# Windowed attention feeding an ELU feed-forward layer: pieces of attention moved to other tiles of a chunk

## The chip, the cores and the metric

The kernel runs on one core of a Trainium2 chip. Its time is the device time of one execution in microseconds (us); the figure that is compared is the median over several runs. The engines of the core work side by side, each through its own instructions in order: PE (matrix products), DVE and POOL (elementwise work), ACT (functions and copies), SP (issues the transfers).

## What is computed

Eight batches of eight heads, 576 positions of 64 numbers each. Four heads attend to the last 32 positions, four to every fourth of the last 128. The attention's result, 4608 tokens of 512 numbers, goes through two matrix products with an ELU between them.

```python
scores = scale * np.matmul(q, k.transpose(0, 1, 3, 2))
scores = np.where(masks[None, :, :, :], scores, -1000000000.0)
scores = scores - np.max(scores, axis=-1, keepdims=True)
attn = np.exp(scores)
attn = attn / (np.sum(attn, axis=-1, keepdims=True) + 1e-09)
attn_out = np.matmul(attn, v)                       # (8, 8, 576, 64)
x = attn_out.transpose(0, 2, 1, 3).reshape(4608, 512)
h = x @ w_in                                        # 512 x 2048
g = np.where(h > 0.0, h, np.exp(np.minimum(h, 0.0)) - 1.0)
return g @ w_out                                    # 2048 x 512
```

## The kernel before

**Chunks and tiles.** The tokens are worked off in nine chunks of 512 (loop over `c`), the hidden layer in 16 tiles of 128 (loop over `f`). For one tile PE forms `h` (`gemm1`: 12 matmuls of 128x512; from chunk 1 on each operand is split into a rounded part and a remainder, `xh`/`xl` and `wh`/`wl`, and three of the four products are taken), then ACT and DVE make the ELU (`elu`, lines 324 to 342), then PE adds the tile's share of the output (`gemm2`, another 12 matmuls into four `o_ps` banks). `gemm2` runs two tiles behind `gemm1` (`LAG`).

**The ELU of a tile**, in the order of its dependences: ACT copies `h` out of its PSUM bank (L328), ACT takes the exponential (L330), DVE clamps (L336) and combines (L337), ACT rounds to `gh` (L340), DVE takes the remainder `gl` (L341). In chunks 1 to 6 there is one PSUM bank for `h` (`h0`), so the next tile's `gemm1` waits for the copy in L328; the bank `h1` takes results of attention.

**Attention beside it.** A batch has four pairs of heads. Chunk `c` reads tokens of batches `c-1` and `c` at most, so the attention of batch `c+1` is done beside chunk `c`. Batch 0 comes first of all and batch 1 beside chunk 0. From batch 2 on it comes in pieces (`piece`, line 277): at the tiles of a table, `when`, right behind the tile's `gemm1`, PE takes the output products of the pair before (24 small matmuls with `pt` and `vt`) and then the scores of the next pair (72 small matmuls with `kt` and `qt`). `probabilities` (line 245) makes of the scores, in this order: masked sum and maximum on DVE (L253 to L255), six exponentials on ACT, then, in a second step that is emitted one tile later (line 457), six more exponentials (all L259), the sum's reciprocal on DVE (L181, L182), the scaling on POOL (L183), and six transposes on DVE (L265) that fill `pt`. All of `pt` must be there before the output products of that pair can run, at the next piece. ACT copies these into `x32` (L173, L176). The last piece of a chunk completes the last pair of batch `c+1` and takes the scores of batch `c+2`'s first pair.

**Between chunks.** `split_x(c+1)` makes `xh` on ACT (L302) and `xl` on DVE (L303) out of `x32`, eight instructions on each engine. They write the same tiles that the chunk before reads, so the first can start when PE has used `xh` for the last time, in the last tile's `gemm1`, and the next chunk's first `gemm1` waits for them. Only one `gemm2` lies between. The first two `elu` of a chunk share ACT with the copies of the chunk before's output (`store`, L355), which empty the `o_ps` banks. In chunk 1, `split_w` splits weights beside the first tiles (L132 on DVE).

**The order of the work.** PE keeps the order in which the program is written. On ACT, DVE, POOL and SP a scheduler orders the instructions by its own estimate of when each can start; `tc.issue_after(x)` makes it put what follows no earlier than `x`. The order is fixed before the kernel runs.

Of the kernel before, what the change touches and what calls it, by code (L numbers as in the profile page):

```python
# [18 lines left out]
B, H, S, D = 8, 8, 576, 64  # L19
# [27 lines left out]
def body(ctx: ExitStack, tc: tile.TileContext, q, k, v, masks, w_in, w_out, out):  # L47
# [36 lines left out]
    def load_w(k, behind=None):  # L84

        raw[k] = wst.tile([P, 2, DM], I64, name=f"r{k % NR}")
        if behind is not None:
            nc.gpsimd.tensor_copy(out=raw[k].bitcast(F32)[:QB, :, 0:1], in_=behind[:, 0:2].unsqueeze(2))
        for t in range(2):
            i = need[2 * k + t]  # L90
            nc.sync.dma_start(out=raw[k][:, t, :], in_=(w_in, w_out)[i % 2][i // 2])
# [6 lines left out]
    def magnitude(k):  # L98
        pair = full2[k] = wst.tile([P, 2, DM], F32, name=f"a{k}")
        for t in range(2):  # L100
            full[need[2 * k + t]] = pair[:, t, :]
        return nc.scalar.activation(out=pair.rearrange("p t c -> p (t c)"), in_=halves(k)[1].bitcast(F32), func=AF.Abs)

    def convert(k, keep=lambda ins: ins, part=slice(0, 2 * DM)):

        lo, hi = [u[:, part] for u in halves(k)]
        a = full2[k].rearrange("p t c -> p (t c)")[:, part]
        au = a.bitcast(U32)

        keep(nc.vector.tensor_scalar(out=a, in0=a, scalar1=TINY, scalar2=None, op0=ALU.max))  # L110

        keep(nc.vector.tensor_scalar(out=au, in0=au, scalar1=0x07FFFFFF, scalar2=3, op0=ALU.bitwise_and, op1=ALU.logical_shift_left))  # L112
        keep(nc.vector.scalar_tensor_tensor(out=au, in0=hi, scalar=0xC0000000, in1=au, op0=ALU.bitwise_and, op1=ALU.bitwise_or))  # L113

        return keep(nc.vector.scalar_tensor_tensor(out=au, in0=lo, scalar=29, in1=au, op0=ALU.logical_shift_right, op1=ALU.bitwise_or))  # L115

    def split_w(k):

        if k >= K0:
            both = wst.tile([P, 2, 2, DM], F32R, name=f"r{k - K0}")  # L120
            h, l = both[:, 0, :, :], both[:, 1, :, :]
        else:
            l = wst.tile([P, 2, DM], F32R, name=f"a{k - 1}")
            slot = NF - K0 + k // 2
            if slot < NR:
                if k % 2 == 0:
                    split_w.room = wst.tile([P, 2, 2, DM], F32R, name=f"r{slot}")
                h = split_w.room[:, k % 2, :, :]
            else:
                h = wst.tile([P, 2, DM], F32R, name=f"a{K0 + k - 2 * (NR - NF + K0)}")  # L130
        nc.scalar.copy(out=h, in_=full2[k])  # L131
        nc.vector.tensor_tensor(out=l, in0=full2[k], in1=h.bitcast(F32), op=ALU.subtract)  # L132
        for t in range(2):
            wh[need[2 * k + t]], wl[need[2 * k + t]] = h[:, t, :], l[:, t, :]
# [157 lines left out]
    def split_x(c):  # L292
        for hp in range(NC):
            xh[hp] = xp.tile([P, TC], F32R, name=f"xh{hp}")
            xl[hp] = xp.tile([P, TC], F32R, name=f"xl{hp}")
            t0 = c * TC
            while t0 < (c + 1) * TC:
                b, o = divmod(t0, S)
                n = min(S - o, (c + 1) * TC - t0)
                u = slice(t0 - c * TC, t0 - c * TC + n)  # L300
                src = x32[b][:, hp, o:o + n]
                nc.scalar.copy(out=xh[hp][:, u], in_=src)  # L302
                nc.vector.tensor_tensor(out=xl[hp][:, u], in0=src, in1=xh[hp][:, u].bitcast(F32), op=ALU.subtract)  # L303
                t0 += n
# [14 lines left out]
    def gemm1(c, f):  # L319
        for h_ps in first if (c, f) == (0, 0) else product1(c, f):  # L320
            pass
        return h_ps

    def elu(h_ps, first):
        e = fp.tile([P, TC], F32, name="e", bufs=3)
        if not first:
            h = fp.tile([P, TC], F32, name="h", bufs=1)
            freed.append(nc.scalar.copy(out=h, in_=h_ps).ins)  # L328
            h_ps = h
        nc.scalar.activation(out=e, in_=h_ps, func=AF.Exp)  # L330
        if first:
            below.append(nc.scalar.activation(out=e, in_=e, func=AF.Relu, scale=-1.0, bias=1.0).ins)
            g = fp.tile([P, TC], F32, name="gh", bufs=3)
            hidden.append(nc.vector.scalar_tensor_tensor(out=g, in0=h_ps, scalar=0.0, in1=e, op0=ALU.max, op1=ALU.subtract).ins)
            return g, None
        nc.vector.tensor_scalar(out=e, in0=e, scalar1=1.0, scalar2=-1.0, op0=ALU.min, op1=ALU.add)  # L336
        hidden.append(nc.vector.scalar_tensor_tensor(out=e, in0=h_ps, scalar=0.0, in1=e, op0=ALU.max, op1=ALU.add).ins)  # L337
        gh = fp.tile([P, TC], F32R, name="gh", bufs=3)
        gl = fp.tile([P, TC], F32R, name="gl", bufs=2)
        nc.scalar.copy(out=gh, in_=e)  # L340
        nc.vector.tensor_tensor(out=gl, in0=e, in1=gh.bitcast(F32), op=ALU.subtract)  # L341
        return gh, gl
# [15 lines left out]
    def batch_attention(b):  # L358

        x32[b] = xp.tile([P, NPAIR, S], F32, name="x32", bufs=2)  # L360

        old = None
        for hp in range(NPAIR):
            *_, new = probabilities(b, hp, loaded_pairs.pop((b, hp)), banks())
            yield
            if old is not None:
                outputs(*old[:2], [(a, i * NA, (i + 1) * NA) for i, a in enumerate(banks())], *old[2:])
                yield
            old = new
        outputs(*old[:2], [(a, i * NA, (i + 1) * NA) for i, a in enumerate(banks())], *old[2:])  # L370
        yield
# [45 lines left out]
    def flush(n):  # L417
        while len(pend) > n:
            c, f, g = pend.pop(0)
            if f == 0:  # L420
                o_of[c] = [ps_o.tile([P, DM], F32, name="o_ps") for _ in range(TC // P)]
            gemm2(o_of[c], g, f)
            if f == NF - 1:
                store(c, o_of.pop(c))

    for c in range(NCH):
        if c == 1:
            with tc.issue_after(hidden[F0 - 4]), tc.issue_after(below[F0 - 4]):
                split_x(c)
        elif c > 1:  # L430
            split_x(c)
        att = batch_attention(c + 1) if c == 0 else iter(())

        when = () if c == 0 or c >= B - 1 else (0, 4, 7, 11, 14) if c == 1 else (2, 6, 10, 14)
        emitted = 0
        for f in range(NF):
            while c == 0 and ready < min(NF, f + AHEAD):
                with tc.issue_after(below[-1] if below else last_copy.ins):
                    magnitude(ready)
                with tc.issue_after(last_conversion.ins):  # L440
                    last_conversion = convert(ready)
                if ready + NR < NF:
                    load_w(ready + NR)
                ready += 1
            if c == 0 and f == F0 - 4:
                with tc.issue_after(hidden[-1]), tc.issue_after(below[-1]):
                    split_x(0)
            if c == 0 and K0 <= f + 2 < NF:
                with tc.issue_after(hidden[-1]):
                    split_w(f + 2)  # L450
            while c == 1 and split < min(K0, f + 2):

                with tc.issue_after(hidden[NF - 4 if split < 2 else NF - 1]):
                    split_w(split)
                split += 1
            pend.append((c, f, elu(gemm1(c, f), c == 0 and f < F0)))
            if steps is not None:

                with tc.issue_after(freed[-1]):
                    current, steps = next(steps), None  # L460
            if f in when:
                n = (c + 1) * NPAIR + when.index(f) + NPAIR + 1 - len(when)
                current, steps = None, piece(current, divmod(n, NPAIR) if n < B * NPAIR else None)
            while emitted < (f + 1) * STEPS // (NF - 1):
                emitted += 1
                if c == 0 and emitted <= 2:
                    with tc.issue_after(last_step[NPAIR - 1]):
                        next(att, None)
                else:
                    next(att, None)  # L470
            flush(LAG)
# [60 lines left out]
```

## Time and profile before

| | |
|---|---|
| time, median of 3 runs | 922.26 us (921.44 to 922.37) |
| the profiled execution's own time | 921.04 us |
| its span, first to last instruction | 919.3 us |
| PE busy | 889.4 us (97%) |
| DVE busy | 553.1 us (60%) |
| ACT busy | 463.2 us (50%) |
| POOL busy | 45.9 us (5%) |
| mean granted PE clock | 0.996 |
| a tile's `gemm1` or `gemm2`, 12 matmuls, on the chain of waits | 2.72 us |

A row of the timeline reads: start in the span, duration (both us), engine, line of the program, operation, what it writes and reads, shapes, the number of instructions merged in the row, and in brackets how long the engine stood idle before it and what ended that. A row of waits reads: who waited, for whom, the total in us, how many times, the longest. A row of stretches reads: the stretch in us, its length, the busy time and instructions of PE, PE's weight loads, DVE, ACT and POOL, the granted PE clock, the transfers' share and GB/s. Chunk 2 begins at 242.56 us, chunk 6 at 637.88, chunk 7 at 735.84.

### The profile page before, as it was taken

The page shows a single profiled execution, that of the slowest core. Times are in us where ns is not written, and L with a number is a line of the kernel's source. Part 1 is how long each engine was busy: PE and PEld are TensorE (multiplying, and loading weights), DVE is VectorE, ACT ScalarE, POOL GpSimd, SP SyncE. Part 2 cuts the span into 40 slices and gives each one's busy share as a digit, 9 for nine tenths or more (in the row PEclk, how much of TensorE's full clock was granted, in tenths as well). Part 3 has the DMA queues.
Part 4 walks back from the last instruction along what each step waited for, and adds up shares of the span by engine and source line. Part 5 has one row for each costly group of instructions (what it writes and reads, how often), then busy time and mean ns, then how long its engine had stood idle before and what let it go on. Part 6 is the DMA issues. An engine that isn't in the chain of part 4 may idle for free.

```text
span 919.3 us, 16120 instructions
## 1 busy us (share of the span) xinstructions
PE 889.4 (97%) x6536; PEld 694.0 (75%) x6536; DVE 553.1 (60%) x926; ACT 463.2 (50%) x1317; POOL 45.9 (5%) x36
## 2 busy tenths in 40 slices
PE   6899999999999999999999999999999999999998
PEld 4444467788788877888788878887888888888886
DVE  5999989675755565666655665556555633343332
ACT  4754596455555455444644465455554443344333
POOL 2000000100000000000000000000000000000000
PEclk8999999999999999999999999999999999999999
DMA  9963111111121112111111112111200010001001
GB/s 348 404 231 116 44 36 57 60 45 45 45 90 45 45 44 91 45 45 45 55 37 44 46 44 90 45 44 45 90 19 1 1 47 1 0 1 47 1 1 46
DMA packets 23803, 59.40 MB, mean 65 GB/s; under 512 B 2640, under 2 KB 2736, under 8 KB 23728
## 3 DMA queue, kind: packets, MB, share of 16 engines
q1 hardware_dynamic: 23728, 58.37, 18.7%
q8 instruction: 51, 0.84, 0.4%
q14 instruction: 24, 0.20, 0.1%
HBM read 48.92 MB, written 9.44 MB: 63 GB/s over the span
## 4 chain that ended last, share of the span: by engine, by line
PE 77%; DVE 10%; ACT 6%; DMA 3%; issue 2%; SPq 1%; DVEq 0%; ACTq 0%
PE h L82 38%; PE o_ps L82 36%; PE a_ps L82 3%; ACT sm L259 2%; DMA r<-w_out 2%; DVE a L115 1%; ACT xh L302 1%; DVE a L113 1%; DVE e L336 1%; ACT r L131 1%; DMA kt<-k 1%; DVE a L110 1%; DVE pt L265 1%; DMA vt<-v 1%; DVE a L112 1%
## 5 line engine op out<-in xcount | busy, mean ns | idle before, releaser
L82 PE MATMUL o_ps<-a,gh 128*128 128x512 f32 x576 | 205.7, 426 | 0.0
L82 PE MATMUL o_ps<-r,gh 128*128 128x512 f32 x576 | 193.1, 394 | 1.6 <-ACT o L355 1.3
L340 ACT CAST gh<-e 128x512 fp32r<-128x512 f32 x132 | 82.2, 623 | 221.2 <-DVE e L337 221.2
L82 PE MATMUL h<-xh,r 128*128 128x512 f32 x512 | 183.6, 393 | 5.5 <-ACT xh L302 4.4
L336 DVE TENSOR_SCALAR e<-e 128x512 f32<-128x512 f32 x132 | 62.8, 475 | 161.8 <-ACT e L330 159.7
L82 PE MATMUL h<-xl,r 128*128 128x512 f32 x368 | 143.9, 391 | 5.8 <-DVE xl L303 5.8
L82 PE MATMUL h<-xh,a 128*128 128x512 f32 x480 | 147.8, 389 | 0.0
L82 PE MATMUL o_ps<-r,gl 128*128 128x512 f32 x368 | 143.5, 390 | 1.5 <-DVE gl L341 1.5
L328 ACT COPY h<-h 128x512 f32<-128x512 f32 x132 | 77.1, 584 | 133.2 <-PE h L82 133.2
L82 PEld LDWEIGHTS o_ps<-a,gh 128*128 128x128 f32 x576 | 107.3, 188 | 39.0 <-issue 19.6
L259 ACT ACTIVATE sm<-sm,nmx 96x64 f32<-96x64 f32 x336 | 112.4, 337 | 42.2 <-DVE nmx L255 42.2
L341 DVE TENSOR_TENSOR gl<-e,gh 128x512 fp32r<-128x512 f32 x132 | 91.4, 692 | 69.5 <-ACT gh L340 56.5
L82 PEld LDWEIGHTS o_ps<-r,gh 128*128 128x128 f32 x576 | 107.5, 188 | 25.8 <-ACT o L355 1.7
L82 PEld LDWEIGHTS h<-xh,r 128*128 128x128 f32 x512 | 96.1, 188 | 28.4 <-ACT xh L302 6.5
L337 DVE SCALAR_TENSOR_TENSOR e<-h,e 128x512 f32<-128x512 f32 x132 | 112.0, 849 | 4.3
L82 PEld LDWEIGHTS h<-xh,a 128*128 128x128 f32 x480 | 90.1, 188 | 18.7
L330 ACT ACTIVATE e<-h 128x512 f32<-128x512 f32 x144 | 90.4, 628 | 21.2 <-PE h L82 18.7
L265 DVE STREAM_TRANSPOSE pt<-sm 32x384 f32<-32x384 f32 x168 | 95.4, 568 | 1.9
L82 PEld LDWEIGHTS h<-xl,r 128*128 128x128 f32 x368 | 69.1, 188 | 22.4 <-DVE xl L303 7.7
L82 PEld LDWEIGHTS o_ps<-r,gl 128*128 128x128 f32 x368 | 69.1, 188 | 16.7 <-DVE gl L341 1.9
L183 POOL TENSOR_TENSOR sm<-sm,sums 96x768 f32<-96x768 f32 x24 | 39.9, 1661 | 654.7 <-ACT e L330 403.2
L259 ACT ACTIVATION_READ_ACCUMULATOR sm<-sm,nmx 96x1 f32 x336 | 63.3, 188 | 0.0
(92 smaller groups left out, 764.1 us busy)
## 6 DMA issues: line engine op xcount, KB each, us to landing
vt<-v SPq DMA_DIRECT2D x30, 384.0 KB, 3.2
kt<-k SPq DMA_DIRECT2D x30, 304.0 KB, 4.6
qt<-q SPq DMA_DIRECT2D x30, 288.0 KB, 4.2
r<-w_in SPq DMA_DIRECT2D x16, 512.0 KB, 7.9
r<-w_out SPq DMA_DIRECT2D x16, 512.0 KB, 8.2
out<-o SPq DMA_DIRECT2D x32, 256.0 KB, 2.2
out<-xl SPq DMA_DIRECT2D x4, 256.0 KB, 2.1
r<-v SPq DMA_DIRECT2D x2, 384.0 KB, 8.4
```

What stands on the lines that cost most here:

```text
L82: inorder(nc.tensor.matmul(*args, **kw))
L110: keep(nc.vector.tensor_scalar(out=a, in0=a, scalar1=TINY, scalar2=None, op0=ALU.max))
L112: keep(nc.vector.tensor_scalar(out=au, in0=au, scalar1=0x07FFFFFF, scalar2=3, op0=ALU.bitwise_and, op1=ALU.logical_shift_left))
L183: return keep(eng.tensor_tensor(out=sm, in0=sm, in1=sums.unsqueeze(2).broadcast_to([QB, 2 * NU, 2 * G]), op=ALU.mult))
L259: nc.scalar.activation(out=sm[:, u, :], in_=sm[:, u, :], func=AF.Exp, bias=nmx[:, u:u + 1], scale=0.125, accum_out=sums[:, u:u + 1])
L265: nc.vector.transpose(out=tr[ks, :, cs], in_=sm[cs, :, rs])
L328: freed.append(nc.scalar.copy(out=h, in_=h_ps).ins)
L330: nc.scalar.activation(out=e, in_=h_ps, func=AF.Exp)
L336: nc.vector.tensor_scalar(out=e, in0=e, scalar1=1.0, scalar2=-1.0, op0=ALU.min, op1=ALU.add)
L337: hidden.append(nc.vector.scalar_tensor_tensor(out=e, in0=h_ps, scalar=0.0, in1=e, op0=ALU.max, op1=ALU.add).ins)
L340: nc.scalar.copy(out=gh, in_=e)
L341: nc.vector.tensor_tensor(out=gl, in0=e, in1=gh.bitcast(F32), op=ALU.subtract)
```

## The change

The table of tiles changes: in chunk 1 from 0, 4, 7, 11, 14 to 0, 4, 7, 10, 12, and in chunks 2 to 6 from 2, 6, 10, 14 to 2, 5, 9, 12. The second step of chunk 1's first piece is emitted at tile 2 in place of tile 1. No instruction is added or dropped.

```diff
@@ -431,7 +431,7 @@
-        when = () if c == 0 or c >= B - 1 else (0, 4, 7, 11, 14) if c == 1 else (2, 6, 10, 14)
+        when = () if c == 0 or c >= B - 1 else (0, 4, 7, 10, 12) if c == 1 else (2, 5, 9, 12)
@@ -454,7 +454,7 @@
             pend.append((c, f, elu(gemm1(c, f), c == 0 and f < F0)))
-            if steps is not None:
+            if steps is not None and (c, f) != (1, 1):
 
                 with tc.issue_after(freed[-1]):
                     current, steps = next(steps), None
```

**ACT where chunk 1 meets chunk 2.** `xh` rows are the split for chunk 2, `sm` rows exponentials of the last piece, the `h` row the copy of tile 15. Before:

```order
 L340 CAST gh<-e 128x512
 L259 ACTIVATE sm,sums<-sm,nmx 96x64 x6
 L302 CAST xh_2346<-x_557 128x128
 L302 CAST xh_2346<-x_1582 128x384
 L302 CAST xh_2352<-x_557 128x128
 L302 CAST xh_2352<-x_1582 128x384
 L302 CAST xh_2358<-x_557 128x128
 L302 CAST xh_2358<-x_1582 128x384
 L328 COPY h<-h_2290 128x512
 L259 ACTIVATE sm,sums<-sm,nmx 96x64 x6
 L302 CAST xh_2364<-x_557 128x128
```

Now, on the same engine at the same place:

```order
 L340 CAST gh<-e 128x512
 L302 CAST xh_2346<-x_557 128x128
 L302 CAST xh_2346<-x_1582 128x384
 L302 CAST xh_2352<-x_557 128x128
 L302 CAST xh_2352<-x_1582 128x384
 L302 CAST xh_2358<-x_557 128x128
 L302 CAST xh_2358<-x_1582 128x384
 L328 COPY h<-h_2311 128x512
 L302 CAST xh_2364<-x_557 128x128
 L302 CAST xh_2364<-x_1582 128x384
 L330 ACTIVATE e<-h 128x512
```

Both groups of exponentials have left; they stand beside tiles 12 and 13 now. The same holds where chunks 2 to 6 begin the next one, but for the end of chunk 6, whose last piece has no scores.

**ACT in chunk 1 between its last two pieces.** The `sm` rows are the exponentials of the last piece but one, the `x` row at the end copies out the products of that same pair, which need its `pt`. Before, tiles 11 to 14:

```order
 L259 ACTIVATE sm,sums<-sm,nmx 96x64 x6
 L330 ACTIVATE e<-h 128x512
 L340 CAST gh<-e 128x512
 L328 COPY h<-h_2154 128x512
 L330 ACTIVATE e<-h 128x512
 L340 CAST gh<-e 128x512
 L328 COPY h<-h_2189 128x512
 L173 COPY x_1582<-a_ps_2212 128x96
```

Now, tiles 10 to 12:

```order
 L259 ACTIVATE sm,sums<-sm,nmx 96x64 x6
 L330 ACTIVATE e<-h 128x512
 L340 CAST gh<-e 128x512
 L328 COPY h<-h_2119 128x512
 L330 ACTIVATE e<-h 128x512
 L173 COPY x_1582<-a_ps_2142 128x96
```

One tile's ELU fewer stands between the exponentials and the copy of the products that depend on them.

**ACT in the first tiles of chunk 1.** The `o` row empties the output banks of chunk 0; the second `sm` row before is the moved step. Before:

```order
 L259 ACTIVATE sm,sums<-sm,nmx 96x64 x6
 L330 ACTIVATE e<-h 128x512
 L259 ACTIVATE sm,sums<-sm,nmx 96x64 x6
 L355 COPY o<-o_ps 128x512 x4
 L340 CAST gh<-e 128x512
 L328 COPY h<-h_1476 128x512
 L330 ACTIVATE e<-h 128x512
```

Now:

```order
 L259 ACTIVATE sm,sums<-sm,nmx 96x64 x6
 L330 ACTIVATE e<-h 128x512
 L355 COPY o<-o_ps 128x512 x4
 L340 CAST gh<-e 128x512
 L328 COPY h<-h_1455 128x512
 L259 ACTIVATE sm,sums<-sm,nmx 96x64 x6
 L330 ACTIVATE e<-h 128x512
```

The second six exponentials have moved behind the output copies, tile 1's `gh` and the copy of tile 2's `h`.

**DVE in the same tiles**, from tile 1's `gl` to tile 2's `gl`; the transposes are the first piece's. Before:

```order
 L341 TENSOR_TENSOR gl<-e,gh 128x512
 L336 TENSOR_SCALAR e<-e 128x512
 L265 STREAM_TRANSPOSE pt_79<-sm 32x12x32 x6
 L337 SCALAR_TENSOR_TENSOR e<-h,e 128x512
 L341 TENSOR_TENSOR gl<-e,gh 128x512
```

Now:

```order
 L341 TENSOR_TENSOR gl<-e,gh 128x512
 L181 TENSOR_SCALAR sums<-sums 96x12
 L182 RECIPROCAL sums<-sums 96x12
 L336 TENSOR_SCALAR e<-e 128x512
 L337 SCALAR_TENSOR_TENSOR e<-h,e 128x512
 L265 STREAM_TRANSPOSE pt_79<-sm 32x12x32 x6
 L341 TENSOR_TENSOR gl<-e,gh 128x512
```

The six transposes have moved from ahead of tile 2's L337 to behind it, and the sum's reciprocal from ahead of tile 1's `gl` to behind it.

## The prediction

> **What bounds the kernel now.** PE is busy for 889.4 of 919.3 us, so a move of work between the other engines can only change what PE waits. I read the list of PE's waits first (us in total, times, longest):
>
> ```profile
> PE h L82 <- DVE xl L303: 5.8, 5, 1.2
> PE h L82 <- ACT xh L302: 4.4, 5, 0.9
> PE o_ps L82 <- ACT o L355: 1.3, 1, 1.3
> PE h L82 <- ACT h L328: 1.1, 1, 1.1
> ```
>
> Ten waits at the starts of `gemm1` are for `xh` and `xl`, so they lie where chunks meet; the two single ones lie in chunk 1. The timeline shows a meeting of chunks, 5 with 6:
>
> ```profile
> 637.88 0.39 PE L82 MATMUL h<-xh,r 128*128 128x512 f32 x1
> 640.27 0.49 PE L82 MATMUL h<-xh,r 128*128 128x512 f32 x1 [0.87 <-ACT xh L302]
> 641.96 0.50 PE L82 MATMUL h<-xl,r 128*128 128x512 f32 x1 [1.20 <-DVE xl L303]
> 643.23 0.62 PE L82 MATMUL o_ps<-r,gh 128*128 128x512 f32 x2
> ...
> 637.00 0.35 ACT L259 ACTIVATE sm<-sm,nmx 96x64 f32<-96x64 f32 x1
> 639.00 0.50 ACT L302 CAST xh<-x 128x384 fp32r<-128x384 f32 x1
> ```
>
> Chunk 6's first `gemm1` lasts from 637.88 to 643.23, 5.35 us, with 2.07 us of waits in it. The six exponentials of the last piece's second step (from 637.00) stand on ACT ahead of the last casts to `xh` (from 639.00), for which PE waits. Chunk 6's own last piece has no scores, and so no exponentials. Where it meets chunk 7 the same rows read:
>
> ```profile
> 735.84 0.39 PE L82 MATMUL h<-xh,r 128*128 128x512 f32 x1
> 738.56 0.62 PE L82 MATMUL o_ps<-r,gh 128*128 128x512 f32 x2
> ...
> 732.64 1.94 ACT L302 CAST xh<-x 128x448 fp32r<-128x448 f32 x6 [3.02 <-PE h L82]
> 734.48 0.58 ACT L328 COPY h<-h 128x512 f32<-128x512 f32 x1
> 734.96 0.71 ACT L302 CAST xh<-x 128x448 fp32r<-128x448 f32 x2
> ...
> 735.56 0.76 DVE L303 TENSOR_TENSOR xl<-x,xh 128x448 fp32r<-128x448 f32 x2 [0.22 <-ACT xh L302]
> ```
>
> That `gemm1` takes 738.56 - 735.84 = 2.72 us. With ACT free, the casts begin 3.20 us ahead of it, and the last `xl` ends at 736.32, well before PE's eighth matmul, which reads it. So a meeting loses 5.35 - 2.72 = 2.63 us, and for 2.07 us of idle time in the list. Scaled to the list's 10.2 us over five meetings (into chunks 2 to 6), 10.2 x 2.63 / 2.07 = 13.0 us are lost.
>
> **The meetings of chunks.** The last piece moves from tile 14 to 12. What its chain does with four free tiles behind it is seen on chunk 6's piece beside tile 10:
>
> ```profile
> 703.46 0.97 PE L82 MATMUL a_ps<-kt,qt 64*32 64x64 f32 x72
> 723.55 0.39 PE L82 MATMUL h<-xh,r 128*128 128x512 f32 x1
> ...
> 707.12 0.35 ACT L259 ACTIVATE sm<-sm,nmx 96x64 f32<-96x64 f32 x1 [1.55 <-DVE nmx L255]
> 710.69 0.35 ACT L259 ACTIVATE sm<-sm,nmx 96x64 f32<-96x64 f32 x1
> 720.87 0.62 ACT L340 CAST gh<-e 128x512 fp32r<-128x512 f32 x1 [3.42 <-DVE e L337]
> 721.39 0.58 ACT L328 COPY h<-h 128x512 f32<-128x512 f32 x1
> ...
> 713.42 1.68 POOL L183 TENSOR_TENSOR sm<-sm,sums 96x768 f32<-96x768 f32 x1 [22.37 <-ACT e L330]
> ...
> 713.81 1.84 DVE L337 SCALAR_TENSOR_TENSOR e<-h,e 128x512 f32<-128x512 f32 x1
> 715.57 3.47 DVE L265 STREAM_TRANSPOSE pt<-sm 32x384 f32<-32x384 f32 x6
> 719.08 0.69 DVE L341 TENSOR_TENSOR gl<-e,gh 128x512 fp32r<-128x512 f32 x1
> ```
>
> From the start of the scores (703.46) the first exponentials follow at 3.66 us, the second six at 7.23, POOL's scaling at 9.96, the transposes from 12.11 to 15.58; the rounding to `gh` two tiles on comes at 17.41, ACT's next instruction at 17.93, and the `gemm1` of the tile four further on at 20.09. For a piece beside tile 12, "four further on" is the next chunk's first tile and the `gh` is tile 14's, behind which the order now has the casts. So they start at 17.93, 2.16 us ahead of that `gemm1`, not 3.20 as into chunk 7: the transposes hold DVE until 15.58, and with it tile 14's ELU. From the first cast, chunk 7's rows give 734.48 + 0.58 - 732.64 = 2.42 us to the end of tile 15's copy of `h` and 736.32 - 732.64 = 3.68 us to the last `xl`. That is 20.35 and 21.61. The single `h0` bank is then free 0.3 us late; the eighth matmul, 7 x 0.227 = 1.59 us after the start (2.72 / 12 each), finds its `xl`. I keep 0.3 us a meeting: 5 x 0.3 = 1.5 us stay, **11.5 us go**. The ends: all 13.0 go (as into chunk 7), or none (as now).
>
> **The gaps of three tiles.** From tile 2 to 5 and from 9 to 12 pieces now follow each other after three tiles in place of four, in chunk 1 from 7 to 10 too. Chunk 1 has such a gap from 4 to 7 already:
>
> ```profile
> 171.90 0.97 PE L82 MATMUL a_ps<-kt,qt 64*32 64x64 f32 x72
> ...
> 189.36 0.39 PE L82 MATMUL a_ps<-pt,vt 128*64 128x96 f32 x4
> ...
> kt<-k SPq DMA_DIRECT2D x30, 304.0 KB, 4.6
> ```
>
> From the scores to the next piece pass 17.46 us. The chain wants 15.58, so 1.88 us are spare, and no wait of PE on `pt` stands in that place in the list. I cost the twelve gaps at nothing; what covers them is two tiles' matmuls, and each us by which the chain grew over 1.88 would cost a us in each. No transfer is added; a pair's loads on SP's queue go out with the piece before, land in a median of 4.6 us (last row, the slowest of the three), and keep at least two tiles, 10.9 us. POOL has one scaling a pair, as before.
>
> **The gap of two tiles.** Chunk 1's last two pieces stand beside tiles 10 and 12. A tile is 2 x 2.72 = 5.44 us, so from the scores to the next piece pass 17.46 - 5.44 = 12.02 us, where the chain wants 15.58. PE's output products wait for the last transpose, and PE, in order, holds everything behind them: scores, `gemm2`, the next `gemm1`. That is a new **stall of 3.6 us**, late for all that follows. Nothing in the order shortens it: the same waits for tile 11's copy of `h`, for POOL (L337 takes 1.84 us beside it) and for six transposes remain. Without every wait it would be 3.66 + 4.0 for twice six exponentials (12 x 0.33) + 0.4 for L181 and L182 + 1.68 + 3.47 = 13.2, a stall of 1.2, which is the low end.
>
> **The clock.** Near the start PE once stood idle for about as long:
>
> ```profile
> 14.26 2.19 PE L82 MATMUL c<-ident,sm 96*64 96x96 f32 x24 [3.57 <-DVE sm L183]
> ...
> 9.10:12.51 3.41, 1.59 (x93) 1.04 (x81) 3.05 (x6) 1.69 (x2) 0.18 (x1) 1.00 1.05 415
> 12.51:15.93 3.42, 1.67 (x22) 1.71 (x24) 3.35 (x5) 0.36 (x1) 0.18 (x1) 0.50 1.02 400
> 15.93:19.34 3.41, 3.41 (x91) 2.44 (x90) 3.25 (x7) 3.09 (x10) 1.91 (x2) 0.50 1.05 393
> 244.62:248.03 3.41, 1.85 (x7) 1.31 (x8) 3.40 (x5) 0.90 (x2) 1.25 (x1) 1.00 0.02 5
> ```
>
> These are stretches between changes of the granted clock (the column before the last two). In the first, PE was busy for 1.59 of 3.41 us, 47%; then the clock was 0.50 for two stretches, the second of them fully busy, and 1.00 again. A stretch 54% busy at 244.62 left it at 1.00. If the limit lies between, a stall of 3.6 us is enough wherever it falls: split evenly over two stretches it leaves 1.8 us idle in each, 47% busy. Then a stretch of 3.41 us runs at half speed, which costs 1.7 us less half of what the stall itself still fills of it, 0 to 1.8 us. I take **1.3 us**; the ends are 0 and 3.4 (two stretches).
>
> By the Trainium skill (TensorE: Matmul & The Clock Gate, "Part 1: The HAM clock gate") the clock falls only after about 3.4 us in which PE idles a whole window. By that a 3.6 us stall fills a window in 1 of 20 positions and this term is 0 as a rule, the time 912.4. The row at 9.10 speaks against it, since the clock fell after a window that was not idle.
>
> **The first tiles of chunk 1.**
>
> ```profile
> 155.61 0.33 ACT L259 ACTIVATE sm<-sm,nmx 96x64 f32<-96x64 f32 x1
> 157.60 2.00 ACT L355 COPY o<-o_ps 128x512 f32<-128x512 f32 x4
> ...
> 158.08 0.68 DVE L337 SCALAR_TENSOR_TENSOR e<-h,e 128x512 f32<-128x512 f32 x1
> 162.39 3.47 DVE L265 STREAM_TRANSPOSE pt<-sm 32x384 f32<-32x384 f32 x6
> ...
> 158.22 0.50 PE L82 MATMUL o_ps<-r,gh 128*128 128x512 f32 x1 [1.29 <-ACT o L355]
> 167.77 0.50 PE L82 MATMUL h<-xh,r 128*128 128x512 f32 x1 [1.08 <-ACT h L328]
> ```
>
> The second six exponentials start at 155.61 and the output copies behind them at 157.60, so `o_ps` came late (1.29 us). Moved behind, they let the copies start at 155.61, and the first, 0.62 us long to PE's start, is done before PE asks at 158.22 - 1.29 = 156.9: that wait goes. Tile 1's `gh` is then bound by L337, which ends at 158.76; 0.52 us later (as 720.87 to 721.39) ACT copies `h`, to 159.9, where PE, which goes on from 156.8, wants the bank at 156.8 + 2.72 = 159.5: 0.4 stay. The exponentials follow 0.5 us into that copy, at 159.8, and from there the chain above holds: L337 of tile 2 ends 715.65 - 710.69 = 4.96 us later, at 164.8, no longer behind transposes that end at 165.86. Then `gh` and, 0.52 later, the copy of `h` to 165.9, where PE wants the bank at 165.4: 0.5 stay. Tile 4's `gemm1` starts at 165.95, not 167.77. With the shorter restart **2.0 us go**. The transposes end 8.35 us after 159.8, at 168.2, and the piece beside tile 4 begins at 165.95 + 2.81 = 168.8: 0.6 to spare. The ends: 0 and 2.4 (both waits whole).
>
> **The sum**, against the profiled execution's own 921.04 us: -11.5 - 2.0 + 3.6 + 1.3 = -8.6, so 912.4. The median of the runs shown is 1.2 above that execution, so the forecast is **913.7 us** (47%).
>
> **The rivals.**
>
> *The clock holds* (25%). As forecast without the 1.3: 912.4 us. For it: beside the stall stand matmuls of 512 columns, where the idle time at 14.26 lay among small ones; against it the 47% above. The Trainium skill's rule on the clock gate (TensorE: Matmul & The Clock Gate, Part 1) gives this time.
>
> *The chain closes up* and the stall beside tile 12 is at its low end, 1.2 us, too short for the clock (a stretch stays 65% busy): 922.26 - 11.5 - 2.0 + 1.2 = 910.0 us (10%). Against it: ACT waits for PE's tile 11 between the two sixes, whatever else moves.
>
> *The casts slide further* (12%). If tile 14's ELU comes another us later (DVE holds it behind transposes), each meeting keeps 1.3 us: 913.7 + 5 = 918.7. For it: the slack of the last `xl` is only 21.99 - 21.61 = 0.4.
>
> *Slower: the chain outgrows three tiles* (4%). The place is the output products beside tiles 5 and 12 of chunks 2 to 6, ten new gaps. It decides from a chain longer than 17.46; to eat the 8.6 us and 1.8 more it must cost 1.0 us in each, a chain of 18.5 against 15.58: 913.7 + 10.4 = 924.1. For it: L337 already stretches from 0.68 to 1.84 us beside POOL; against it, the gap of 4 to 7 ran without a wait.
>
> *The meetings stay as they are* (2%), PE waiting for the bank instead of for `xl`: 13.0 remain, chunk 1's 2.0 go and 4.9 come: 925.2, or 921.5 with the stall at its low end.
>
> **Range and chances.** 910.3 to 917.8 us holds the forecast, the clock that holds, and the nearer part of the casts and of the closed-up chain. About 0.2%, 1.8 us, is what a measurement of this kernel can tell from no change. Faster by more 0.94, within it 0.02, slower 0.04.
>
> **What would show it.** Right: the list of PE's waits without the pair for `xh` and `xl`; first `gemm1` of chunks 2 to 6 about 3.0 us long or beginning 0.3 us late behind an ACT `h`; one wait of some 3.6 us of `a_ps` on DVE `pt` beside chunk 1's tile 12, and a second row of granted clock 0.5 soon after it; no wait on `pt` in chunks 2 to 6. Wrong: waits on `pt` at every gap of three tiles, no long one in chunk 1, or `xl` still in the list with several us.

## The result and the profile after

The changed kernel takes 915.45 us in the median of four runs (914.04 to 916.74), against 922.12 us before: a ratio of 0.9929, 95% interval 0.9911 to 0.9946. The forecast was 913.7 us, in a range of 910.3 to 917.8. The profiled execution took 916.74 us, 4.3 less than the one before; its span is 915.0 us, its mean granted clock 0.991.

PE's list of waits after the change, for the places that the prediction speaks of (us in total, times, longest):

```profile
PE a_ps L82 <- issue: 3.6, 1, 3.6
...
PE o_ps L82 <- DVE gl L341: 1.5, 1, 1.5
PE a_ps L82 <- ACT x L176: 1.2, 1, 1.2
PE h L82 <- ACT h L328: 0.5, 3, 0.2
```

The ten waits for `xh` and `xl` are gone, and so are the single ones of 1.3 and 1.1 us in chunk 1. New are one of 3.6 us and one of 1.2 us, both at pieces of chunk 1. The profile names no releaser for the first and writes "issue"; the rows around it do:

```profile
221.37 3.47 DVE L265 STREAM_TRANSPOSE pt<-sm 32x384 f32<-32x384 f32 x6
...
224.94 0.59 PE L82 MATMUL a_ps<-pt,vt 128*64 128x96 f32 x4 [3.59 <-issue]
227.06 1.52 PE L82 MATMUL a_ps<-kt,qt 64*32 64x64 f32 x72
```

DVE's last transpose for that pair ends at 221.37 + 3.47 = 224.84, and PE's output products beside tile 12 start at 224.94, after 3.59 us of idle time.

The meeting of chunks 2 and 3, in PE's, ACT's and DVE's rows:

```profile
345.69 0.50 PE L82 MATMUL h<-xh,r 128*128 128x512 f32 x1 [0.15 <-ACT h L328]
348.59 0.62 PE L82 MATMUL o_ps<-r,gh 128*128 128x512 f32 x2
...
342.70 0.62 ACT L340 CAST gh<-e 128x512 fp32r<-128x512 f32 x1 [3.41 <-DVE e L337]
343.22 1.94 ACT L302 CAST xh<-x 128x192 fp32r<-128x192 f32 x6
345.07 0.57 ACT L328 COPY h<-h 128x512 f32<-128x512 f32 x1
345.54 0.71 ACT L302 CAST xh<-x 128x192 fp32r<-128x192 f32 x2
...
343.96 2.82 DVE L303 TENSOR_TENSOR xl<-x,xh 128x192 fp32r<-128x192 f32 x8
```

The casts start at 343.22, behind tile 14's `gh`, the copy of tile 15's `h` ends at 345.64, and chunk 3's first `gemm1` starts at 345.69. It lasts 348.59 - 345.69 = 2.90 us, not 5.35. The other four meetings look the same, with 2.85 to 2.90 us.

The 1.2 us stand beside tile 7, between the output products and the scores of that piece (DVE, ACT, PE):

```profile
183.99 3.47 DVE L265 STREAM_TRANSPOSE pt<-sm 32x384 f32<-32x384 f32 x6
...
189.28 0.62 ACT L340 CAST gh<-e 128x512 fp32r<-128x512 f32 x1 [3.41 <-DVE e L337]
189.80 0.58 ACT L328 COPY h<-h 128x512 f32<-128x512 f32 x1
190.28 0.24 ACT L176 COPY x<-a_ps 128x96 f32<-128x96 f32 x1
...
190.57 0.97 PE L82 MATMUL a_ps<-kt,qt 64*32 64x64 f32 x72 [1.15 <-ACT x L176]
```

The scores of a piece go into the PSUM bank that holds part of its output products. PE had those products done, but could not start the scores before ACT had copied them out (190.28 + 0.24). ACT came to that copy late, behind tile 6's `gh` and tile 7's `h`, because DVE's transposes had run to 187.46.

The granted clock, as stretches of the execution between its changes (length, then busy time of PE, its weight loads, DVE, ACT, POOL; the granted clock stands before the last two columns):

```profile
131.48:134.90 3.42, 1.58 (x9) 0.96 (x6) 3.42 (x4) 3.42 (x6) 0.00 (x0) 1.00 0.42 120
134.90:138.31 3.41, 3.41 (x9) 2.65 (x9) 2.23 (x5) 2.20 (x5) 0.00 (x0) 0.50 0.00 0
220.23:223.64 3.41, 1.12 (x5) 0.58 (x4) 3.37 (x5) 1.73 (x3) 0.67 (x1) 1.00 0.00 0
223.64:227.06 3.42, 2.12 (x24) 1.92 (x24) 2.90 (x6) 0.24 (x1) 0.00 (x0) 0.50 0.00 0
227.06:230.47 3.41, 3.41 (x79) 2.85 (x78) 1.71 (x3) 1.08 (x2) 0.00 (x0) 0.50 0.53 149
```

After the first 30 us it fell twice: behind the stretch at 131.48 (46% busy), in chunk 0's last tiles, and behind the one at 220.23 (33% busy), which holds most of the stall of 3.6 us.

### The profile page after: what moved, and what is told of

Read it like the earlier page. It is cut to its first block, busy times and chain, and to the rows that moved or that the text cites. A ratio compares the mean times of both kernels' runs of the same rounds, so it can differ in the third digit from the quotient of the medians.

```text
span 915.0 us, 16120 instructions
## 1 busy us (share of the span) xinstructions
PE 891.9 (97%) x6536; PEld 698.0 (76%) x6536; DVE 553.6 (61%) x926; ACT 462.1 (51%) x1317; POOL 46.3 (5%) x36
## 4 chain that ended last, share of the span: by engine, by line
PE 72%; DVE 14%; ACT 7%; DMA 4%; issue 3%; SPq 0%; ACTq 0%; DVEq 0%
PE h L82 35%; PE o_ps L82 33%; PE a_ps L82 3%; DVE pt L265 3%; DMA r<-w_out 2%; DVE e L337 2%; ACT sm L259 2%; DVE a L115 1%; DVE a L113 1%; ACT xh L302 1%; DVE a L132 1%; ACT r L131 1%; ACT h L328 1%; DMA r<-w_in 1%; DVE a L110 1%
## 5 line engine op out<-in xcount | busy, mean ns | idle before, releaser
L336 DVE TENSOR_SCALAR e<-e 128x512 f32<-128x512 f32 x132 | 56.2, 426 | 150.7 <-ACT e L330 148.3
L337 DVE SCALAR_TENSOR_TENSOR e<-h,e 128x512 f32<-128x512 f32 x132 | 119.0, 902 | 4.5
L181 DVE TENSOR_SCALAR sums<-sums 96x12 f32<-96x12 f32 x32 | 6.0, 189 | 108.9 <-ACT sm L259 108.7
```

## The experiments

Ratios are to the kernel before, run on the same chip beside each.

| kernel | median us | ratio, 95% interval |
|---|---|---|
| changed kernel | 915.45 | 0.9929, 0.9911 to 0.9946 |
| changed kernel once more | 915.81 | 0.9929, 0.9914 to 0.9944 |
| chunk 1 at its old tiles | 914.72 | 0.9911, 0.9893 to 0.9929 |
| second step at tile 1 again | 916.81 | 0.9938, 0.9919 to 0.9956 |
| chunks 2 to 6 at their old tiles | 925.49 | 1.0035, 1.0018 to 1.0052 |
| fifteen gaps of two tiles (one run) | 992.41 | |
| 0, 4, 8, 11, 14 and 2, 5, 8, 11 | 912.17 | 0.9888, 0.9873 to 0.9903 |
| no scores in the last piece | 909.83 | 0.9863, 0.9847 to 0.9879 |
| twelve exponentials at once | 915.14 | 0.9921, 0.9900 to 0.9941 |

### The changed kernel once more

> The changed kernel once more, beside the next three on one chip. 914.0 to 916.7 us as before; half clock behind the stall beside chunk 1's tile 12 again.

915.81 us (915.69 to 916.38). In its profiled execution (span 914.0 us) the clock held at the end of chunk 0, and the first tiles of chunk 1 show what stays of the two waits there:

```profile
160.42 0.50 PE L82 MATMUL h<-xh,r 128*128 128x512 f32 x1 [0.32 <-ACT h L328]
166.42 0.50 PE L82 MATMUL h<-xh,r 128*128 128x512 f32 x1 [0.26 <-ACT h L328]
```

The prediction had 0.4 and 0.5 us of delay at these two `gemm1`. Measured as the length of the `gemm2` before each, they are 3.20 - 2.72 = 0.5 and 3.15 - 2.72 = 0.4 us. From the `gemm2` of chunk 0 that starts at 132.29 us (131.82 before) to the piece beside tile 4 pass 37.09 us, 1.85 less than before (predicted: 2.0).

### Chunk 1 at its old tiles

```diff
-(0, 4, 7, 10, 12) if c == 1 else (2, 5, 9, 12)
+(0, 4, 7, 11, 14) if c == 1 else (2, 5, 9, 12)
```

> Chunk 1 keeps its old tiles 0, 4, 7, 11, 14 (no gap of two tiles); all else is the changed kernel. Theory (the gap of two tiles is dear: a stall of 3.6 us plus up to 2.3 us of half clock behind it, against 2.1 us that the freed meeting of chunks 1 and 2 saved): 915.4 - 3.6 - (0 to 2.3) + 2.1 = 911.6 to 913.9, no PE wait over 2 us and no half clock after 200 us. Rival (the stall costs little, since ACT and DVE catch up in it what they would lose later): 915.4 + 2.1 = 917.5.

914.72 us (913.30 to 915.99), 0.8 over the theory's upper number; its interval overlaps the changed kernel's. The stall of 3.6 us is gone, so the rival's 917.5 is out. But the meeting of chunks 1 and 2 waits again (0.9 and 1.2 us), and in the profiled execution the clock fell behind these waits, so that this `gemm1` took 6.13 us where it took 5.39 before the change. The theory had expected no half clock there; 0.7 of the 0.8 us are lost in this `gemm1` alone:

```profile
243.56:246.97 3.41, 1.30 (x5) 0.53 (x5) 3.05 (x6) 1.27 (x5) 1.47 (x1) 1.00 0.00 0
246.98:250.39 3.41, 3.41 (x10) 2.63 (x9) 3.34 (x7) 1.83 (x3) 0.00 (x0) 0.50 0.02 5
```

So the gap of two tiles bought about as much as it cost, as far as the intervals tell: with it, a stall and its half clock; without it, 2.6 us at the meeting and, as here, half clock as well.

### The second step at tile 1 again

```diff
-            if steps is not None and (c, f) != (1, 1):
+            if steps is not None:
```

> The changed tiles, but the first piece's second exponentials at tile 1 again. Theory: the two waits in chunk 1's first tiles come back (1.3 and 1.1 us) and the wait of 1.2 us for ACT's copy beside tile 7 goes, since the piece beside tile 4 finds ACT on time: about +1.2, 916.6. Rival (the step's place does not matter, the gain there is only a shift): 915.4, the wait beside tile 7 still there.

916.81 us, ratio 0.9938: the expected number, though the interval does not tell it from the changed kernel's. The profile decides (PE's rows):

```profile
168.54 0.50 PE L82 MATMUL h<-xh,r 128*128 128x512 f32 x1 [1.09 <-ACT h L328]
190.09 0.39 PE L82 MATMUL a_ps<-pt,vt 128*64 128x96 f32 x4
191.34 0.90 PE L82 MATMUL a_ps<-kt,qt 64*32 64x64 f32 x66
```

The wait for tile 3's copy of `h` is back (1.09 us; that for the output copies at 0.38, since the clock had fallen at the end of chunk 0 and PE came later), and the scores beside tile 7 follow their products after 1.25 us with no wait. In the changed kernel's first profile the clock had fallen at the end of chunk 0 too, so the two can be set side by side: here the piece beside tile 4 starts 1.9 us later than there (171.48 against 169.60), the scores beside tile 7 only 0.8 (191.34 against 190.57). The moved step gains in the first tiles and pays most of it back beside tile 7.

### Chunks 2 to 6 at their old tiles

```diff
-(0, 4, 7, 10, 12) if c == 1 else (2, 5, 9, 12)
+(0, 4, 7, 10, 12) if c == 1 else (2, 6, 10, 14)
```

> Chunks 2 to 6 keep tiles 2, 6, 10, 14; chunk 1 is the changed one. Theory (each meeting keeps 0.5 us in place of 2.6 when the last piece stands at tile 12): the four meetings into chunks 3 to 6 lose 4 x 2.1 = 8.4 again, ten gaps of three tiles give back 0.1 each: 915.4 + 7.4 = 922.8. Rival (most of the gain came from chunk 1): 915 to 918.

925.49 us, slower than the kernel before, by 0.18 to 0.52%. The rival is out: the gain lies in chunks 2 to 6, and chunk 1's part of the change, its table and the moved step, by itself loses. It is 2.7 us over the theory's number. Four meetings wait again, beside the stall of the gap of two tiles:

```profile
PE h L82 <- DVE xl L303: 4.6, 4, 1.2
PE a_ps L82 <- issue: 3.6, 1, 3.6
PE h L82 <- ACT xh L302: 3.5, 4, 0.9
```

Besides, a first `gemm1` of a chunk took 6.32 us (chunk 3's, from 344.26) where the others took 5.27 to 5.36: half clock from 348.42 on, behind a stretch that was 40% busy. From start to start chunk 3 takes 100.4 us and chunks 4 and 5 take 98.8, so this half clock cost 1.6 of the 2.7 us; the rest is not accounted for. Over its seven runs the mean clock is 0.986 to 0.996. That meetings can cost half clock too was not in the theory.

### Fifteen gaps of two tiles

```diff
-(0, 4, 7, 10, 12) if c == 1 else (2, 5, 9, 12)
+(0, 4, 7, 11, 14) if c == 1 else (2, 4, 6, 8)
```

> Chunk 1 at its old tiles, chunks 2 to 6 at tiles 2, 4, 6, 8: fifteen gaps of two tiles. Theory A (each stalls PE for 3.6 us, and the clock halves behind each, since one stretch of 3.41 us is then under half busy): from about 912.5 for no such gap, + 15 x (3.6 + 1.3 to 2.3) = 986 to 1001, half clock behind nearly every stall. Rival B (the stall alone; the clock falls only after a stretch that is wholly idle): 912.5 + 15 x 3.6 = 966.5, half clock after one stall or none. By the Trainium skill (TensorE: Matmul & The Clock Gate, Part 1: The HAM clock gate) the clock falls after an idle window of about 3.4 us, which is B.

992.41 us, inside theory A and 26 over B. PE's waits in front of the output products, and six of the stretches:

```profile
PE a_ps L82 <- issue: 54.2, 15, 3.9
...
382.44:385.85 3.41, 2.11 (x10) 1.41 (x8) 3.35 (x5) 1.14 (x3) 1.66 (x1) 1.00 0.00 0
385.85:389.26 3.41, 1.12 (x24) 1.05 (x24) 3.31 (x7) 0.83 (x2) 0.00 (x0) 1.00 0.00 0
389.26:392.67 3.41, 3.41 (x80) 2.83 (x78) 2.26 (x4) 1.09 (x2) 0.00 (x0) 0.50 0.54 138
...
419.98:423.39 3.41, 1.09 (x5) 0.56 (x3) 3.37 (x5) 1.73 (x3) 0.65 (x1) 1.00 0.00 0
423.40:426.81 3.41, 2.14 (x28) 1.95 (x29) 2.86 (x5) 0.24 (x1) 0.00 (x0) 0.50 0.02 5
426.81:430.22 3.41, 3.41 (x79) 2.85 (x78) 1.74 (x3) 1.08 (x2) 0.00 (x0) 0.50 0.52 144
```

Fifteen waits come to 54.2 us, 3.6 each. Against some 913.3 us without such gaps (912.17 of the run with tiles 2, 5, 8, 11, and the 1.1 us that this kernel waits beside tile 7), a gap costs (992.4 - 913.3) / 15 = 5.3 us: 3.6 of stall, and 1.7 that are left for the half clock. The clock fell behind all fifteen, in ten places for one stretch (as in the first rows: 33% busy, then fully), in five for two (32%, then 63%, then fully). In four of the ten the stall filled a whole stretch (0 to 2% busy); the other eleven fell behind stretches that were 13 to 43% busy, which rival B does not allow.

### Four tiles after the first piece, three after the others

```diff
-(0, 4, 7, 10, 12) if c == 1 else (2, 5, 9, 12)
+(0, 4, 8, 11, 14) if c == 1 else (2, 5, 8, 11)
```

> Chunk 1 at tiles 0, 4, 8, 11, 14, chunks 2 to 6 at 2, 5, 8, 11. Theory (the gap of 4 to 7 cost 1.2 us because ACT came late after the first piece; a last piece beside tile 11 leaves DVE free in time, so the 0.5 us that stay at a meeting go): no PE wait beside chunk 1's second and third piece, first gemm1 of chunks 3 to 6 without a wait, chunk 2's still with 2.6 us: 3.2 us under the run with chunk 1's old table, 911.5. Rival (the 0.5 us come from ACT's order and stay): 913.5, with 0.3 us for ACT's copy of h at those meetings.

912.17 us, ratio 0.9888, faster than the changed kernel and 0.7 us over the expected number. PE's waits:

```profile
PE o_ps L82 <- DVE gl L341: 1.5, 1, 1.5
PE h L82 <- DVE xl L303: 1.2, 1, 1.2
...
PE h L82 <- ACT xh L302: 0.9, 1, 0.9
PE h L82 <- ACT h L328: 0.6, 2, 0.3
```

The wait for ACT's copy beside the second piece is gone, and of the five meetings only the one into chunk 2 waits, for `xl` and `xh`; the clock fell behind that wait here too. The two waits for `h` lie in chunk 1's first tiles. With the last piece beside tile 11 nothing stays of the 0.5 us at a meeting, so it was DVE's transposes beside tile 14 that kept it, not ACT's order: ACT does the same work in the same order there, and the casts for chunk 3 start at 338.73, 3.20 us ahead of its `gemm1`, as those into chunk 7 did before. Some 0.5 of the 0.7 us are the third gap of three tiles that each of chunks 2 to 6 now has: it delays the scores by 0.1 us, and the expectation left it out.

### No scores in the last piece

```diff
-(0, 4, 7, 10, 12) if c == 1 else (2, 5, 9, 12)
+(0, 4, 8, 11, 14) if c == 1 else (2, 5, 8, 11, 14)
...
-                n = (c + 1) * NPAIR + when.index(f) + NPAIR + 1 - len(when)
-                current, steps = None, piece(current, divmod(n, NPAIR) if n < B * NPAIR else None)
+                n = (c + 1) * NPAIR + when.index(f)
+                current, steps = None, piece(current, divmod(n, NPAIR) if f != when[-1] else None)
```

> Each of the chunks 1 to 6 takes its batch whole: a fifth piece, beside tile 14, without scores, as chunk 6 has it, and the next batch's first scores in the next chunk's first piece (tiles 0, 4, 8, 11, 14 and 2, 5, 8, 11, 14). Theory (a meeting is lost to the last piece's exponentials and transposes, not to its products): no wait at any meeting, no stall, no half clock after 200 us: 921.0 - 13.0 - 2.0 + 18 gaps x 0.1 = 907.8 of the profiled kind, 908.5 in the median. Rival (the copies of products beside tile 14 delay the casts as well): 2.6 us at each meeting, 918 and more.

909.83 us (909.13 to 910.71), ratio 0.9863: the fastest here, 0.65% under the changed kernel's median on the same chip. All of PE's waits behind the attention of batch 0:

```profile
PE o_ps L82 <- DVE gl L341: 1.5, 1, 1.5
...
PE h L82 <- DVE gh L334: 0.9, 1, 0.9
...
PE o_ps L82 <- ACT gh L340: 0.4, 1, 0.4
PE a_ps L82 <- ACT x L173: 0.2, 1, 0.2
```

All four lie in chunk 0. No meeting waits, though a piece stands beside tile 14 in each chunk. A last piece there costs nothing so long as it brings no scores, and so no exponentials and transposes into the meeting. The profiled execution (909.54 us) is 1.7 us over its expectation of 907.8. Of these 0.6 are the clock at the end of chunk 0, which fell there behind the 1.5 us wait for `gl`: the piece beside tile 4 comes that much later than in the second profile of the changed kernel. The fifth piece has a price as well: chunks 3 to 5 take 96.8 us each from start to start, and 96.5 with pieces at 2, 5, 8, 11. What this kernel gains over the one with those pieces comes from the meeting of chunks 1 and 2, which no longer waits.

### Twelve exponentials at once

```diff
+                if (c, f) == (1, 10):
+                    current, steps = next(steps), None
```

(behind the call of `piece`)

> The changed kernel, but the piece beside chunk 1's tile 10 takes its twelve exponentials at once. Theory (the chain is 15.6 us long because the second six stand behind ACT's copy of tile 11, which waits for PE): the second six start 1.7 us earlier, the stall beside tile 12 falls from 3.6 to 1.5 to 1.9 us, the stretch stays over half busy and the clock at 1.00 there; 911.5 to 913. Rival (the chain's length is set by POOL and the transposes): stall 3.6 and half clock as before, 915.4.

915.14 us. The rows around the stall (ACT, DVE, PE):

```profile
217.73 0.57 ACT L328 COPY h<-h 128x512 f32<-128x512 f32 x1
218.33 0.64 ACT L330 ACTIVATE e<-h 128x512 f32<-128x512 f32 x1
...
219.00 1.22 DVE L336 TENSOR_SCALAR e<-e 128x512 f32<-128x512 f32 x1 [0.71 <-ACT e L330]
220.86 3.47 DVE L265 STREAM_TRANSPOSE pt<-sm 32x384 f32<-32x384 f32 x6
...
224.43 0.59 PE L82 MATMUL a_ps<-pt,vt 128*64 128x96 f32 x4 [2.52 <-issue]
```

The stall is 2.5 us, between the two theories, and the stretch with it was 37% busy, so the clock fell all the same. The twelve exponentials end 1.3 us earlier, but tile 11's copy of `h` and its exponential stand behind them on ACT now, and on DVE tile 11's L336, which waits for that exponential (0.71 us idle), stands ahead of the transposes. The chain is as long as the ELU of the tile beside it makes it, on both engines, not only ACT's wait for PE.

## Why the prediction was right, and which of its terms were off

The terms, in us against the profiled execution before. The last column takes the second profile of the changed kernel (span 914.0 against 919.3), in which the clock held at the end of chunk 0.

| term | predicted | measured |
|---|---|---|
| five meetings of chunks, with the gaps of three tiles but for 4 to 7 | -11.5 | -10.0 |
| first tiles of chunk 1 | -2.0 | -1.85 |
| gap from tile 4 to 7 | 0 | +1.1 |
| stall beside tile 12 | +3.6 | +3.6 |
| half clock behind it | +1.3 | +1.4 (2.3 in the first profile) |
| all before chunk 0's last tiles (the start differs so from run to run) | 0 | +0.5 |
| sum | -8.6 | -5.3 |

**The meetings.** The reading of chunk 6's two ends held to 0.1 us: the casts start behind tile 14's `gh` and the `h0` bank is 0.3 us late. The term was mis-sized by what the 0.3 us bring with them. PE's restart makes that `gemm1` 0.1 to 0.2 us longer (2.85 to 2.90), so 0.5 stay and not 0.3, and each gap of three tiles delays the scores by 0.1. A chunk with both takes 96.8 us from piece to piece beside tile 2, 2.0 less than before, where 2.3 was the forecast.

**The gaps of three tiles** hold the one step that failed: "1.88 us are spare". That counts the transposes' end against the output products. It leaves out what comes after the transposes on DVE and ACT: the next tile's ELU, and then the copy of the products, for which the scores of the same piece wait. Beside tile 7 this copy was on the limit before the change:

```profile
190.32 0.24 ACT L176 COPY x<-a_ps 128x96 f32<-128x96 f32 x1
...
190.61 0.97 PE L82 MATMUL a_ps<-kt,qt 64*32 64x64 f32 x72
```

It ended at 190.56, and the scores started at 190.61. They followed their products (189.36) by 1.25 us, against 1.14 behind a gap of four tiles, so nothing was spare. In the changed kernel the piece beside tile 4 has a chain 1.1 us longer (transposes to 16.7 us after its scores, not 15.6), since the moved step made ACT late, and PE paid for all of it beside tile 7. The run with 4 to 8 took the wait away, and so did the second step at tile 1, with which the transposes end 15.6 us after the scores again.

**The gap of two tiles** stalled PE for 3.59 us, as worked out. The rival of a chain that closes up, with a stall of 1.2 us, is out.

**The clock.** It fell behind the stall in both profiles. The page of the Trainium skill (TensorE: Matmul & The Clock Gate, Part 1: The HAM clock gate) asks for an idle window of about 3.4 us. In the profiles of these runs it fell 27 times between the first 30 us and the end, behind stretches that were 0 to 46% busy, and only four of these were under 10%; the measurement decides. What the prediction priced, half clock behind one stall, is right. The rival of the clock that holds is out. What the prediction left out is that other waits do the same by chance of where they fall: at the end of chunk 0 (1.5 us for `gl`; in the first profile chunk 1 starts 1.6 us later for it, and 0.6 are left beside tile 4, since the first tiles then wait less) and at a meeting that still waits. The kernel before seems to pay this in some executions too: over the runs beside the experiments it took 921.4 to 924.7 us, with mean clocks of 1.0 to 0.990. Its profiled execution, in which the clock held after the first 30 us, is then a flattering one; no profile on record shows a slower one.

**The median** moved by 6.7 us, the profiled executions by 4.3 and 5.3. The profiled one before was among the fastest of its kernel, and both of the changed one had half clock beside tile 12. So it is in part luck that the median came within 1.8 us of the forecast: the sum of the terms missed the second profile's 915.76 us by 3.4 (912.4).

**The rivals.** That the chain outgrows three tiles has a true core, but in one place, not ten. The casts did not slide further. That the change does not free the meetings is out.

## What to carry to other kernels

When work that feeds a later step moves, do not compare its end with that step alone: follow the in-order engines past it to the last instruction that the step's neighbours wait for, here the copy that empties a shared bank. Where chunks meet, ask what must not be in flight rather than how early the last piece can go; leaving the next batch's scores out of it was worth more than any of the tables of tiles tried here. And a stall of the matrix engine that empties half a stretch of some 3.4 us can bring half clock behind it: here fifteen stalls of 3.6 us cost half as much again.

## What the runs showed of the hardware that was not expected

In all ten profiles the granted clock changed only at multiples of 3.41 us from one another, and going down and coming back had different limits. From 30 us on it fell from full speed behind every stretch that was at most 43% busy, and stayed behind every one that was at least 53% busy; between lie stretches of 44 to 46%: four of them, in the last tiles of chunk 0, were followed by half clock, and three, at the very end of an execution, were not. Coming back took more: after a stretch at half clock that was 52 to 65% busy it stayed at half for another, and after one of 82% or more it returned. With that goes the price of a stall of 3.6 us, 1.4 us of clock in one profile and 2.3 in the other: in the latter the stall's tail and the small matmuls behind it left the first half-speed stretch 62% busy, and a second followed; in the former that stretch was fully busy. The busy share is not all that counts for coming back. In the first 30 us, where the attention of batch 0 runs, half clock stayed behind four stretches that were 78 to 100% busy, and what else decides there is open.
